# Four value loads ahead of the first relayout, and the first two relayouts issued from two queues

## The chip, the cores and the metric

The kernel runs on one core of a Trainium2 chip. The metric is the device time of one execution in microseconds, and a kernel is described by the median of several executions. Before the change that median is 673.52 us over three runs (673.15 to 676.69).

## The reference, cut to what matters

Talking-heads attention feeds two feed-forward blocks; all inputs and outputs are float32.

```
scores = 0.125 * q @ k.T                  # 2 batches, 12 heads, 448 x 448, head size 64
scores = einsum('bhij,hg->bgij', scores, w_pre)       # mixes the 12 heads
attn   = softmax(scores, axis=-1)
attn   = einsum('bhij,hg->bgij', attn, w_post)        # mixes the 12 heads again
x      = (attn @ v)  as 896 tokens x 768
x      = (silu(x @ w_gate) * (x @ w_val)) @ w_out     # 768 -> 1536 -> 768
h      = x @ w_in                                     # 768 -> 2048
y      = (h * clip(h + 3, 0, 6) / 6) @ w_out2         # 2048 -> 768
```

## The kernel before, in words

The attention is worked off in eight tiles `t` of 100 to 120 query rows, four for each batch. For a tile, `scores` multiplies q and k for six pairs of heads (`c` = 0 to 5), and `scores_out` copies the two banks of a pair to a tile `S` in SBUF, one by VectorE (DVE) and one by ScalarE (ACT). In `S` a partition is a query row, and the heads lie beside each other. To mix the heads on TensorE they have to lie on partitions. That is the **relayout**: a DMA inside SBUF takes every twelfth row of `S` and writes each head of such a row to a partition of its own in a tile `sx`. A chunk is ten query rows. `relayout(m)` moves eight of its rows (104 partitions of `sx`, L204, issued by SyncE, called SP here), `relayout_rest(m)` the other two (24 partitions, L220, issued by GpSimd, called POOL). I call them relayout m and rest m. There are 90 chunks, and two chunks make one `sx` tile and one **step** i; 45 steps follow each other. `S` exists twice, so tile 0 is in one and tile 1 in the other.

Step i works on several stages at once: `premix(i+2)` (L239, TensorE multiplies `sx` by the first mixing matrix), `row_max(i+2)` (L252, DVE), `exps(i+1)` (L261, ACT), `weights(i+1)` (L269 to L273, DVE), `postmix(i)` (L287, TensorE), `attn_out(i)` (L306, DVE and ACT), and, spread over the steps, the scores of a later tile, attention times values (`av`, L318 and L337) and loads. The order of the instructions on each engine is the order in which this code is written; nothing reorders it. Each engine works its own list from the front, and an instruction that waits holds all that stands behind it on its engine. A DMA stands in the list of the engine that issues it.

DMAs that SP and ACT issue take eight semaphores in turn, named DMAHW0 to DMAHW7, in the order of the code. A DMA that takes a semaphore waits until the DMA that used it last, eight such DMAs earlier, has landed. POOL's DMAs have eight others (DMASW). `next_engines` is a DMA of a few bytes that POOL issues between groups of four rests.

At the start, q and k of tile 0 are loaded in pieces from SP and ACT, then q of tiles 1 and 2, both mixing matrices (`W1`, `W2`) and the first two of four pieces of the first batch's values (`load_v(0, j)`, L118) from SP. TensorE computes all scores of tiles 0 and 1 (L526 to L536); between the two tiles the code issues relayouts 0 to 7. Then the steps begin at i = -2. The other two value pieces are issued by ACT at the ends of steps 1 and 2, and q of tile 3 (`load_q`, L109) by ACT at the end of step 3. Relayouts 8 and later are placed by the rules in L650 to L657: at most three in a step, no more than a few steps ahead, and only if the tile was scored in an earlier step (`scored`).

Of the kernel before, what the change touches and what calls it, by code (L numbers as in the profile page):

```python
# [16 lines left out]
B, H, S, D = 2, 12, 448, 64  # L17
NT = B * S
DM = H * D
HP = H // 2  # L20
# [7 lines left out]
JC = 4  # L28
# [20 lines left out]
def kernel(  # L49
# [14 lines left out]
    nc = tc.nc  # L64
# [5 lines left out]
    def bank(name, tag):  # L70
        return ps.tile([128, 512], F32, name=name, tag=tag, bufs=BUFS[tag])
# [18 lines left out]
    small = kp.tile([128, 8], F32, name="small")  # L90
# [23 lines left out]
    def new_v(b):  # L114
        vs[b] = pv.tile([128, JC, H, D], F32, name=f"v{b}", tag="v")

    def load_v(b, j, eng=nc.scalar):
        eng.dma_start(  # L118
            out=vs[b][:, j].rearrange("p h d -> p (h d)"), in_=vv[b, :, j * DM : (j + 1) * DM]
        )  # L120
# [15 lines left out]
    nc.sync.dma_start(out=W2.rearrange("p g k -> p (g k)"), in_=w_post)  # L136
    load_q(2, eng=nc.sync)
    new_v(0)
    for j in range(2):
        load_v(0, j, nc.sync)  # L140

    Ss = [psc.tile([128, H + 1, S], F32, name=f"S{i}") for i in range(2)]
# [14 lines left out]
    stiles, pqk = {}, {}  # L157

    def scores(t, c, tags=("pqk", "pqk")):

        b, i = divmod(t, 4)
        n = ROWS[b][i]
        if c == 0:
            stiles[t] = Ss[t % 2]
        base = c * n
        p = [bank(f"pqk{t}_{c}_{e}", tags[e]) for e in range(2)]
        for s in range(2):
            lo, hi = 64 * s, min(64 * s + 64, n)
            for e in range(2):
                r = slice(64 * e, 64 * e + 64)  # L170
                nc.tensor.matmul(  # L171
                    p[e][lo:hi, :S],
                    lhsT=qs[t][r, base + lo : base + hi],
                    rhs=ks[b][r, c, :],
                    start=True,
                    stop=True,
                    tile_position=(64 * e, 64 * s),
                )
        for e in range(2):
            pqk[t, 2 * c + e] = p[e]  # L180

    def scores_out(t, c):
        n = ROWS[t // 4][t % 4]
        for e in range(2):
            h = 2 * c + e
            copy = nc.scalar.copy if e else nc.vector.tensor_copy
            copy(stiles[t][:n, h, :], pqk.pop((t, h))[:n, :S])  # L187

    sx = {}

    in_turn = mybir.DependencyInfo(mybir.DependencyClass.Sync, mybir.DependencyReason.DATA)

    def relayout(m, then=None):

        t, c = chunks[m]
        i, r = divmod(m, 2)  # L200
        if r == 0:
            sx[i] = psx.tile([128, 2, S], F32, name=f"sx{i}", tag="sx")
        rows = stiles[t][c : c + 7 * STRIDE + 1 : STRIDE, :, :]
        dma = nc.sync.dma_start(out=sx[i][0:104, r, :], in_=rows)  # L204
        if then:
            tc.add_manual_dep(dma.ins, then, in_turn, reason="a step's share of the DMA engines")

    def next_engines(n):

        to = 4 + n % 4  # L210
        nc.gpsimd.dma_start(
            out=small[0:24, to : to + 1], in_=small[0:8, 0:3].rearrange("p (h w) -> p h w", w=1)
        )

    next_engines(0)

    def relayout_rest(m):
        t, c = chunks[m]
        rows = stiles[t][c + 8 * STRIDE : c + 9 * STRIDE + 1 : STRIDE, :H, :]
        nc.gpsimd.dma_start(out=sx[m // 2][104:128, m % 2, :], in_=rows)  # L220
        if m % 4 == 3 and m + 1 < NCH:
            next_engines(m // 4 + 1)

# [105 lines left out]
    turns = cst.tile([1, 1], F32, name="turns")  # L329
# [189 lines left out]
    def keep_clock(n):  # L519

        p = ps.tile([128, 512], F32, name=f"clock{n}", tag="ppost", bufs=BUFS["ppost"])
        for _ in range(n):
            nc.tensor.matmul(p[:, :480], lhsT=ones[0], rhs=ones[1], start=True, stop=True)

    keep_clock(WARM)
    placed = 0  # L526
    for t in range(2):
        for c in range(HP):
            scores(t, c, (("pqk", "pqk"), ("ppre", "ppre"), ("ppost", "ppost"), ("ppre", "pav"))[(6 * t + c) % 4])
            scores_out(t, c)  # L530
        if t == 0:
            for _ in range(8):
                relayout(placed)
                relayout_rest(placed)
                placed += 1
    rests = placed  # L536

# [3 lines left out]
    def at_step(i, f, *args, place="end"):  # L541
        extra[i][place].append((f, args))
# [9 lines left out]
        else:  # L552
            at_step(now + 1, scores_out, t, c, place="S")

    scored = {0: -3, 1: -3}
    for t in range(2, 8):
        scored[t] = 6 * t - 7
        for c in range(HP):
            i = scored[t] - 5 + c
# [8 lines left out]
    for t, (begin, end) in enumerate(((5, 10), (11, 16), (17, 22), (23, 28), (29, 34), (35, 40), (41, 46))):  # L568
        busy = None
        for c in range(HP):  # L570
            i = begin + c * (end - begin + 1) // HP
            out = x_out if t < 6 else x_last
# [11 lines left out]
        if t < 6:  # L584
            step = 1 if t < 4 else 2
            i = split_at.setdefault(t, max(end + 1, split_at.get(t - 1, 0) + 4 // step))
# [4 lines left out]
    at_step(20, new_v, 1)  # L591
    for b in range(2):
        at_step(scored[4 * b + 3] + 1, new_x, b)
    loads = [(1, load_v, 0, 2), (2, load_v, 0, 3), (3, load_q, 3), (6, load_q, 4)]
    loads += [(7 + n, load_k, 1, n, n + 1) for n in range(HP)]
    loads += [(15, load_q, 5), (21, load_q, 6), (27, load_q, 7)]
    loads += [(20 + 2 * j, load_v, 1, j) for j in range(JC)]
# [17 lines left out]
    for i in range(-LOOK, NP):  # L615
# [36 lines left out]
        for m in ready[:1]:  # L652
            relayout(m, begun_at)
        run(i, "end")
        for m in ready[1:]:
            relayout(m, maxed)
        placed += len(ready)  # L657

        while rests < placed and rests // 2 <= i + LOOK + 4 and i > scored[chunks[rests][0]]:
            relayout_rest(rests)  # L660
            rests += 1
# [181 lines left out]
```

## Time and profile before

| | |
|---|---|
| median of three runs | 673.52 us |
| the profiled execution, its own time | 671.94 us |
| span in its profile | 670.2 us |
| TensorE busy | 659.1 us (98% of the span) |
| VectorE, ScalarE, GpSimd busy | 499.8, 296.5, 160.4 us |
[...]

The span is the time from the first to the last instruction on the chip. The profiled execution took 1.74 us more than its span, and 1.58 us less than the median. "PE" is TensorE's multiplications and "PEld" its weight loads; "SPq" and "ACTq" are the instructions with which SP and ACT issue DMAs. In a row of the timeline, the bracket says how long the engine stood idle before, and who ended that.

### The profile page before, as it was taken

What the parts mean: (1) busy time and instruction counts of PE and PEld (TensorE: products, weight loads), DVE (VectorE), ACT (ScalarE), POOL (GpSimd) and SP (SyncE); (2) the same over time, 40 slices, a digit from 0 to 9 for tenths busy, and PEclk for the clock granted to TensorE, in tenths of its full rate; (3) what the DMA queues carried; (4) which work ended last, traced back from release to release, by engine and by line L of the source; (5) the groups of instructions that cost most, each with busy time, mean ns of one, the idle gap of its engine ahead of it and who ended that gap; (6) DMA issues with size and microseconds to landing.
All of it is one profiled execution on the core that took longest, in us unless ns stands there. A gap on an engine that the chain in (4) does not pass through costs nothing.

```text
span 670.2 us, 16126 instructions
## 1 busy us (share of the span) xinstructions
PE 659.1 (98%) x6680; PEld 561.8 (84%) x6680; DVE 499.8 (75%) x836; ACT 296.5 (44%) x603; POOL 160.4 (24%) x204
## 2 busy tenths in 40 slices
PE   8999999999999999999999999999999999999997
PEld 2456665666899999999999999999999998999996
DVE  4878888889278888887886666578888888775540
ACT  4567776777244343433432323244445543333220
POOL 3544466545111122111120000013333332000000
PEclk9999999999999999999999999999999999999999
DMA  7767576545024242332432434222223333554420
GB/s 253 218 200 210 178 219 192 181 142 198 3 94 141 95 141 95 112 124 95 135 100 95 132 104 134 102 94 97 94 95 101 119 96 100 178 155 122 145 67 27
DMA packets 35225, 86.87 MB, mean 130 GB/s; under 512 B 10096, under 2 KB 23040, under 8 KB 35152
## 3 DMA queue, kind: packets, MB, share of 16 engines
q1 hardware_dynamic: 21600, 71.43, 32.3%
q10 hardware_dynamic: 5616, 10.48, 5.1%
q0 software_dynamic: 7936, 3.94, 2.4%
q8 instruction: 52, 0.85, 0.6%
q14 instruction: 21, 0.17, 0.1%
HBM read 62.37 MB, written 2.75 MB: 97 GB/s over the span
## 4 chain that ended last, share of the span: by engine, by line
PE 94%; DMA 3%; DVE 2%; ACT 1%; issue 0%; ACTq 0%; SPq 0%; DVEq 0%
PE pi L441 17%; PE pp L441 17%; PE po L441 13%; PE pv L441 12%; PE pg L441 12%; PE pav L318 5%; PE ppost L287 5%; PE ppre L239 4%; PE pqk L171 4%; PE p L441 2%; PE pav L337 2%; DMA sx<-S 2%; DMA k<-in_k_dram 1%; ACT e L261 1%; DVE nm L252 0%
## 5 line engine op out<-in xcount | busy, mean ns | idle before, releaser
L441 PE MATMUL pp<-g,hp 128*128 128x448 f32 x384 | 107.9, 362 | 0.0
L703 POOL TENSOR_TENSOR g<-rl,g 128x448 fp32r<-128x448 f32 x32 | 41.4, 1313 | 167.9 <-ACT g L702 167.9
L441 PE MATMUL po<-u,ho 128*128 128x448 f32 x288 | 81.3, 363 | 0.0
L441 PEld LDWEIGHTS pp<-g,hp 128*128 128x128 f32 x384 | 71.9, 187 | 4.5 <-ACT hp L427 0.2
L261 ACT ACTIVATE e<-ppre,nm 128x448 f32<-128x448 f32 x90 | 56.3, 631 | 35.4 <-DVE nm L252 33.8
L441 PE MATMUL pp<-g,lp 128*128 128x448 f32 x192 | 69.7, 363 | 0.2 <-DVE lp L432 0.2
L441 PE MATMUL pi<-x2l,hi 128*128 128x448 f32 x192 | 69.7, 363 | 0.0
L441 PE MATMUL pi<-x2h,hi 128*128 128x448 f32 x192 | 69.6, 362 | 0.0
L441 PE MATMUL pi<-x2h,li 128*128 128x448 f32 x192 | 69.1, 360 | 0.0
L703 POOL TENSOR_TENSOR u<-sg,u 128x448 fp32r<-128x448 f32 x24 | 32.2, 1362 | 148.3 <-ACT u L702 148.3
L220 POOL DMA_DIRECT2D sx<-S x90 | 52.5, 584 | 49.5 <-issue 11.8
L441 PEld LDWEIGHTS po<-u,ho 128*128 128x128 f32 x288 | 54.1, 188 | 3.5
L252 DVE TENSOR_REDUCE nm<-ppre 128x1 f32<-128x448 f32 x90 | 51.9, 618 | 4.8 <-PE ppre L239 2.3
L287 PE MATMUL ppost<-wn,e 60*64 60x60 f32 x2520 | 51.0, 220 | 3.0 <-DVE wn L273 1.7
L441 PE MATMUL po<-u,lo 128*128 128x448 f32 x144 | 51.8, 360 | 0.0
L318 PEld LDWEIGHTS pav<-at,v 128*64 128x64 f32 x576 | 27.9, 136 | 28.4 <-ACT xs L360 14.2
L239 PE MATMUL ppre<-sx,W 64*64 64x448 f32 x360 | 49.7, 544 | 1.3 <-ACT S L187 0.6
L287 PEld LDWEIGHTS ppost<-wn,e 60*64 60x64 f32 x2520 | 45.1, 134 | 6.1 <-ACT at L306 2.0
L171 PE MATMUL pqk<-k,q 64*64 64x448 f32 (+3 forms) x384 | 47.8, 539 | 1.2 <-DMA k<-in_k_dram 0.6
L441 PE MATMUL pg<-xl,hg 128*128 128x448 f32 x132 | 47.9, 363 | 0.0
L441 PE MATMUL pv<-xl,hv 128*128 128x448 f32 x132 | 47.9, 363 | 0.0
L441 PE MATMUL pg<-xh,hg 128*128 128x448 f32 x132 | 47.8, 362 | 0.0
(98 smaller groups left out, 1399.1 us busy)
## 6 DMA issues: line engine op xcount, KB each, us to landing
sx<-S SPq DMA_DIRECT2D x90, 182.0 KB
ri<-in_moe_w_in_dram SPq DMA_DIRECT2D x16, 768.0 KB
ro<-in_moe_w_out_dram SPq DMA_DIRECT2D x12, 768.0 KB
rg<-in_moe_w_gate_dram SPq DMA_DIRECT2D x11, 768.0 KB
rv<-in_moe_w_val_dram SPq DMA_DIRECT2D x11, 768.0 KB
rp<-in_moe_w_out_dram SPq DMA_DIRECT2D x12, 640.0 KB
rp<-in_moe_w_out_dram SPq DMA_DIRECT2D x6, 768.0 KB
sx<-S POOLq DMA_DIRECT2D x90, 42.0 KB, 4.5
```

The source lines that it names most:

```text
L171: nc.tensor.matmul(p[e][lo:hi, :S], lhsT=qs[t][r, base + lo : base + hi], rhs=ks[b][r, c, :], start=True, stop=True, tile_position=(64 * e ...
L220: nc.gpsimd.dma_start(out=sx[m // 2][104:128, m % 2, :], in_=rows)
L239: nc.tensor.matmul(p[a][64 * r : 64 * r + 64, :S], lhsT=W1[rows, :], rhs=x[rows, r, :], start=True, stop=True, tile_position=(64 * a, 64 * r),
L252: top = nc.vector.tensor_reduce(nm[:, a : a + 1], pre[i][a][:, :S], AX.X, ALU.max, negate=True)
L261: nc.scalar.activation(e2[a], p[a][:, :S], AF.Exp, bias=nm[:, a : a + 1], scale=1.0, accum_out=sm[:, a : a + 1])
L287: mm = nc.tensor.matmul(p[s][64 * c : 64 * c + 64, at, :, :], lhsT=e2[a][rows, 64 * k : 64 * k + 64], rhs=wn[rows, a, :].rearrange("p (g k ...
L318: nc.tensor.matmul(p[64 * e : 64 * e + 64, : 2 * n], lhsT=vs[b][:, jc, h, :], rhs=ats[t][:, 2 * jc : 2 * jc + 2, h, :n], start=jc == 0, st ...
L337: mm = nc.tensor.matmul(pavs[t, c][64 * e : 64 * e + 64, a * n : a * n + n], lhsT=vs[b][rows, JC - 1, h, :], rhs=ats[t][rows, KB - 1, h, : ...
L441: nc.tensor.matmul(p[:, :S], lhsT=wt[:, kk, :], rhs=xx, start=start, stop=stop)
L703: eng.tensor_tensor(to[1], src, to[0].bitcast(F32), ALU.subtract)
```

## The change

All four pieces of the first batch's values are now loaded by SP ahead of the first relayout; the two loads that ACT issued in steps 1 and 2 are gone. Relayout 1 is issued by ACT and rest 0 by SP. The last pair of scores of tile 1 is computed behind the first premix, and its copies stand behind the first exponentials; the relayouts of tile 1 may therefore start only in step 0 and not in step -1. The banks of the scores of tiles 0 and 1 are listed one by one so that the first premix finds free banks. The first `next_engines` moves 16 elements where it moved 24.

```
-    for j in range(2):
+    for j in range(JC):
         load_v(0, j, nc.sync)
...
-    def relayout(m, then=None):
+    def relayout(m, then=None, eng=nc.sync):
...
-        dma = nc.sync.dma_start(out=sx[i][0:104, r, :], in_=rows)
+        dma = eng.dma_start(out=sx[i][0:104, r, :], in_=rows)
...
-    def next_engines(n):
+    def next_engines(n, turns=3):
...
-            out=small[0:24, to : to + 1], in_=small[0:8, 0:3].rearrange("p (h w) -> p h w", w=1)
+            out=small[0 : 8 * turns, to : to + 1], in_=small[0:8, 0:turns].rearrange("p (h w) -> p h w", w=1)
...
-    next_engines(0)
+    next_engines(0, 2)
...
-        nc.gpsimd.dma_start(out=sx[m // 2][104:128, m % 2, :], in_=rows)
+        eng.dma_start(out=sx[m // 2][104:128, m % 2, :], in_=rows)
...
+    banks = [("pqk", "pqk"), ("ppre", "ppre"), ("ppost", "ppost"), ("ppre", "pav"), ("pqk", "pqk"), ("ppre", "ppre")]
+    banks += [("ppost", "ppost"), ("ppre", "pav"), ("pqk", "pqk"), ("ppost", "ppost"), ("pqk", "pqk"), ("ppost", "ppost")]
     for t in range(2):
         for c in range(HP):
-            scores(t, c, (("pqk", "pqk"), ("ppre", "ppre"), ("ppost", "ppost"), ("ppre", "pav"))[(6 * t + c) % 4])
+            if (t, c) == (1, HP - 1):
+                break
+            scores(t, c, banks[6 * t + c])
             scores_out(t, c)
         if t == 0:
             for _ in range(8):
-                relayout(placed)
-                relayout_rest(placed)
+                relayout(placed, eng=nc.scalar if placed == 1 else nc.sync)
+                relayout_rest(placed, eng=nc.sync if placed == 0 else nc.gpsimd)
                 placed += 1
...
-    scored = {0: -3, 1: -3}
+    scored = {0: -3, 1: -1}
+    at_step(-2, scores, 1, HP - 1, banks[-1], place="av2")
+    at_step(-1, scores_out, 1, HP - 1, place="S")
...
-    loads = [(1, load_v, 0, 2), (2, load_v, 0, 3), (3, load_q, 3), (6, load_q, 4)]
+    loads = [(3, load_q, 3), (6, load_q, 4)]
```

SP's list at the start, before the change, with the semaphores that each DMA waits for: two value loads, then relayouts 0 to 3 (two to a tile `sx`).

```order
L109 DMA q2_114<-in_q_dram 128x720 [waits DMAHW4_49]
L118 DMA v0_116<-in_v_dram 128x768 [waits DMAHW5_49]
L118 DMA v0_116<-in_v_dram 128x768 [waits DMAHW6_49]
L204 DMA sx0_187<-S0_119 104x1x448 [waits DVE_49,DMAHW7_49,Activation_49,Pool_49]
L204 DMA sx0_187<-S0_119 104x1x448 [waits DMAHW0_49]
L204 DMA sx1_192<-S0_119 104x1x448 [waits DMAHW1_49]
L204 DMA sx1_192<-S0_119 104x1x448 [waits DMAHW2_49]
```

The same place of SP's list with the change; L220 is rest 0.

```order
L109 DMA q2_114<-in_q_dram 128x720 [waits DMAHW4_49]
L118 DMA v0_116<-in_v_dram 128x768 [waits DMAHW5_49]
L118 DMA v0_116<-in_v_dram 128x768 [waits DMAHW6_49]
L118 DMA v0_116<-in_v_dram 128x768 [waits DMAHW7_49]
L118 DMA v0_116<-in_v_dram 128x768 [waits DMAHW0_49]
L204 DMA sx0_189<-S0_121 104x1x448 [waits DVE_49,DMAHW2_49,Activation_49,Pool_49]
L220 DMA sx0_189<-S0_121 24x1x448 [waits DMAHW3_49]
L204 DMA sx1_194<-S0_121 104x1x448 [waits DMAHW4_49]
L204 DMA sx1_194<-S0_121 104x1x448 [waits DMAHW5_49]
```

Four value loads stand ahead of relayout 0 instead of two, rest 0 stands behind it, and relayout 1 has left for ACT's list.

ACT's list in steps 1 to 3 before the change: `S0` copies of tile 2's scores (L187), the two value loads, q of tile 3 with its semaphore, and the exponentials of steps 3 to 5 (L261).

```order
L118 DMA v0_116<-in_v_dram 128x768
L261 ACTIVATE e2_126,sm3_413<-ppre3_0_389,nm3_395 128x448 [waits DVE_49,Activation_49]
L261 ACTIVATE e3_127,sm3_413<-ppre3_1_390,nm3_395 128x448 [waits DVE_49,Activation_49]
L306 COPY at0_327<-ppost2_1_417 128x84x5 [waits PE_49]
L187 COPY S0_119<-pqk2_1_1_463 120x448 [waits PE_49]
L118 DMA v0_116<-in_v_dram 128x768 [waits DMAHW2_49]
L261 ACTIVATE e0_124,sm4_476<-ppre4_0_453,nm4_459 128x448 [waits DVE_49,Activation_49]
L261 ACTIVATE e1_125,sm4_476<-ppre4_1_454,nm4_459 128x448 [waits DVE_49,Activation_49]
L306 COPY at0_327<-ppost3_1_480 128x84x5 [waits PE_49]
L187 COPY S0_119<-pqk2_2_1_526 120x448 [waits PE_49]
L109 DMA q3_535<-in_q_dram 128x714 [waits DMAHW5_49]
L261 ACTIVATE e2_126,sm5_541<-ppre5_0_516,nm5_522 128x448 [waits DVE_49,Activation_49]
```

The end of the same stretch with the change.

```order
L306 COPY at0_323<-ppost2_1_418 128x84x5 [waits PE_49]
L187 COPY S0_121<-pqk2_1_1_464 120x448 [waits PE_49]
L261 ACTIVATE e0_126,sm4_476<-ppre4_0_454,nm4_460 128x448 [waits DVE_49,Activation_49]
L261 ACTIVATE e1_127,sm4_476<-ppre4_1_455,nm4_460 128x448 [waits DVE_49,Activation_49]
L306 COPY at0_323<-ppost3_1_480 128x84x5 [waits PE_49]
L187 COPY S0_121<-pqk2_2_1_526 120x448 [waits PE_49]
L109 DMA q3_535<-in_q_dram 128x714 [waits DMAHW6_49]
L261 ACTIVATE e2_126,sm5_541<-ppre5_0_516,nm5_522 128x448 [waits DVE_49,Activation_49]
```

The value loads are gone, and q of tile 3 waits for another semaphore. Who held these two semaphores stands in SP's list; before the change, DMAHW5 is relayout 14's, the first of `sx7`:

```order
L204 DMA sx6_344<-S1_120 104x1x448 [waits DMASW2_49,DMAHW3_49,DMASW1_49,PE_49]
L204 DMA sx6_344<-S1_120 104x1x448 [waits DMAHW4_49,DVE_49]
L204 DMA sx7_406<-S1_120 104x1x448 [waits DMASW4_49,DMAHW5_49,DMASW3_49,PE_49]
L204 DMA sx7_406<-S1_120 104x1x448 [waits DMAHW6_49,DVE_49]
L204 DMA sx8_470<-S1_120 104x1x448 [waits DMASW7_49,DMAHW0_49,DMASW6_49,PE_49]
```

With the change, DMAHW6 is relayout 12's, the first of `sx6`, and relayouts 10 to 12 stand together:

```order
L204 DMA sx4_266<-S0_121 104x1x448 [waits DMAHW3_49,DVE_49]
L204 DMA sx5_340<-S1_122 104x1x448 [waits DVE_49,PE_49,DMAHW4_49,Activation_49,Pool_49]
L204 DMA sx5_340<-S1_122 104x1x448 [waits DMAHW5_49,DVE_49]
L204 DMA sx6_343<-S1_122 104x1x448 [waits DMAHW6_49,DMASW1_49]
L204 DMA sx6_343<-S1_122 104x1x448 [waits DMAHW7_49,PE_49]
L204 DMA sx7_407<-S1_122 104x1x448 [waits DMASW3_49,DMAHW0_49,DMASW2_49,DVE_49]
```

So the DMA that q of tile 3 has to wait for is two relayouts earlier than before, and relayouts 10 and 11 now wait for the postmix and the row maximum of a later step (PE and DVE in their waits).

## Rows read from the trace of the kernel before

**Rows 1.** Page, the chain that ended last: shares of the span by engine.

```profile
PE 94%; DMA 3%; DVE 2%; ACT 1%; issue 0%; ACTq 0%; SPq 0%; DVEq 0%
```

**Rows 2.** Busy time by stretch: stretch, its length, busy time (instructions), clock, DMA share, GB/s.

```profile
34.00:170.00 136.00, 132.94 (x3616) 85.87 (x3616) 115.58 (x338) 97.83 (x281) 70.73 (x117) 1.00 0.61 187
170.00:670.00 500.00, 496.03 (x2602) 463.37 (x2600) 362.70 (x451) 181.01 (x283) 74.94 (x58) 1.00 0.33 107
```

**Rows 3.** The chain that ended last, 10 to 38 us: start, us, what.

```profile
11.84 4.36 DMA sx<-S
16.25 0.98 PE ppre L239 x4
17.91 1.35 ACT e L261 x4
...
25.35 7.85 DMA sx<-S
33.23 0.33 ACTq L109
```

**Rows 4.** Timeline of TensorE at the first premix.

```profile
15.26 4.01 PE L239 MATMUL ppre<-sx,W 64*64 64x448 f32 x16 [0.64 <-ACT S L187]
16.25 0.30 PEld L239 LDWEIGHTS ppre<-sx,W 64*64 64x64 f32 x6 [0.83 <-DMA sx<-S]
```

**Rows 5.** DMA engines, 7 to 12.4 us: mean busy tenths in 40 slices; issues and KB.

```profile
DMA  7889999999999999995778979999999664327100
v<-in_v_dram SPq DMA_DIRECT2D x2, 384.0 KB
sx<-S SPq DMA_DIRECT2D x2, 182.0 KB
sx<-S POOLq DMA_DIRECT2D x2, 42.0 KB, 3.6
```

**Rows 6.** DMA engines, 8.4 to 11.4 us: totals; queue: packets, MB, share of 16 engines.

```profile
DMA packets 418, 1.01 MB, mean 336 GB/s; under 512 B 85, under 2 KB 85, under 8 KB 418
q1 hardware_dynamic: 402, 1.01, 96.3%
```

**Rows 7.** DMA engines, 12.4 to 24 us: SP's and ACT's hardware queue.

```profile
q1 hardware_dynamic: 1163, 1.94, 47.1%
```

**Rows 8.** Timeline of SP's issues: relayouts 0 to 17 merged, and relayout 5 alone.

```profile
10.95 19.27 SPq L204 DMA_DIRECT2D sx<-S  x18
15.30 1.12 SPq L204 DMA_DIRECT2D sx<-S  x1
```

**Rows 9.** Timeline of VectorE, steps -2 to 0.

```profile
17.25 1.16 DVE L252 TENSOR_REDUCE nm<-ppre 128x1 f32<-128x448 f32 x2 [1.95 <-PE ppre L239]
19.28 0.17 DVE L269 TENSOR_SCALAR rc<-sm 128x2 f32<-128x2 f32 x1 [0.88 <-ACT e L261]
22.52 1.15 DVE L252 TENSOR_REDUCE nm<-ppre 128x1 f32<-128x448 f32 x2
```

**Rows 10.** Timeline of ScalarE: a copy of tile 1, then steps 2 and 3.

```profile
10.96 0.54 ACT L187 COPY S<-pqk 120x448 f32<-120x448 f32 x1 [0.21 <-PE pqk L171]
...
28.86 0.53 ACT L187 COPY S<-pqk 120x448 f32<-120x448 f32 x1 [0.84 <-PE pqk L171]
28.86 0.34 ACTq L118 DMA_DIRECT2D v<-in_v_dram  x1
29.30 0.63 ACT L261 ACTIVATE e<-ppre,nm 128x448 f32<-128x448 f32 x1
...
31.89 0.53 ACT L187 COPY S<-pqk 120x448 f32<-120x448 f32 x1 [0.77 <-PE pqk L171]
33.97 0.63 ACT L261 ACTIVATE e<-ppre,nm 128x448 f32<-128x448 f32 x1 [1.55 <-DVE at L306]
```

**Rows 11.** Timeline of TensorE at premix 2 and at premix 5.

```profile
20.95 0.97 PE L239 MATMUL ppre<-sx,W 64*64 64x448 f32 x8
29.45 1.22 PE L239 MATMUL ppre<-sx,W 64*64 64x448 f32 x6
```

More of the change, by code (lines that the diff above doesn't have):

```diff
@@ L203, in relayout, with relayout_rest @@
         rows = stiles[t][c : c + 7 * STRIDE + 1 : STRIDE, :, :]
-        dma = nc.sync.dma_start(out=sx[i][0:104, r, :], in_=rows)
+        dma = eng.dma_start(out=sx[i][0:104, r, :], in_=rows)
         if then:
             tc.add_manual_dep(dma.ins, then, in_turn, reason="a step's share of the DMA engines")
-    def next_engines(n):
+    def next_engines(n, turns=3):
         to = 4 + n % 4
         nc.gpsimd.dma_start(
-            out=small[0:24, to : to + 1], in_=small[0:8, 0:3].rearrange("p (h w) -> p h w", w=1)
+            out=small[0 : 8 * turns, to : to + 1], in_=small[0:8, 0:turns].rearrange("p (h w) -> p h w", w=1)
         )
-    next_engines(0)
-    def relayout_rest(m):
+    next_engines(0, 2)
+    def relayout_rest(m, eng=nc.gpsimd):
         t, c = chunks[m]
         rows = stiles[t][c + 8 * STRIDE : c + 9 * STRIDE + 1 : STRIDE, :H, :]
-        nc.gpsimd.dma_start(out=sx[m // 2][104:128, m % 2, :], in_=rows)
+        eng.dma_start(out=sx[m // 2][104:128, m % 2, :], in_=rows)
         if m % 4 == 3 and m + 1 < NCH:
```

## The prediction

> **What bounds the kernel now.** I read the page's chain first: TensorE has 94% of it, DMA 3%, the rest little [rows 1]. The table by stretch then says where TensorE is not the bound: from 34 us on it is busy 132.94 of 136 us and 496.03 of 500 us [rows 2]. So nearly all of what the change can touch lies before 34 us, and a shift of the front there passes on to the end one for one, because behind it an almost unbroken row of TensorE work follows. The chain between 10 and 38 us [rows 3] shows the front's two DMA waits. First, relayout 1 is issued at 11.84 us and holds the chain for 4.36 us; premix 0 runs on from 16.25 us. TensorE could have gone on earlier: it began premix 0 at 15.26 us and its weight loads then stood 0.83 us until the relayout came [rows 4]. Second, a relayout issued at 25.35 us lands 7.85 us later, and what waits is no premix but ACT's load of q for tile 3, at 33.23 us. By the order, that load takes the semaphore of relayout 14 and holds ACT's list until it has landed. Behind it stand the exponentials of step 5, which start at 33.97 us after 1.55 us of idle ACT [rows 5]; the copy before them ended at 31.89 + 0.53 = 32.42 us. The bracket names DVE there, but by the chain the DMA issue came last.
>
> **The value loads ahead of relayout 0 (cost).** Two loads of 384 KB (393,216 bytes each) [rows 6] are added to SP's list ahead of the first relayout. In SP's list they cost nothing: the next thing there waits until 10.95 us for the copies of tile 0 [rows 7], and the semaphores they take were last used by early pieces of q and k. On the DMA engines they cost time. While the first two value loads ran, the queue kept 96.3% of the 16 engines busy at 336 GB/s [rows 8], so two more take 786,432 / 336,000 = 2.34 us. Part of that is free, since the engines run dry before relayout 0 now begins: the last nine slices of 0.135 us up to 12.4 us are busy 6, 6, 4, 3, 2, 7, 1, 0 and 0 tenths, which leaves 6.1 slices, 0.82 us, idle [rows 6]. Net +1.52 us for the data of relayout 0. Bounds: 0, if the relayouts pass the loads without loss, and +2.34 us, if none of the idle time is filled.
>
> **Relayouts 0 and 1 side by side (no gain).** Before, relayout 1 was issued 11.84 - 10.95 = 0.89 us after relayout 0 [rows 3, 7]; now both go at 10.95 us. But from 12.4 to 24 us the queue keeps 47.1% of 16, that is 7.5, engines busy with relayouts alone and moves 1.94 MB [rows 9], or 10.4 relayouts of 182 KB (186,368 bytes): 1.11 us for each. Were the idle half usable by a relayout, the share would not stay at half while SP has the next ones issued. [...] By the rows, the gain lies between 0 and the 0.89 us between the issues; I take 0, since the engines that carry relayouts were full.
>
> **Rest 0 on SP's list.** It stands behind relayout 0 and ahead of relayout 2. By its bytes it adds 42/182 of 1.11 = 0.26 us [rows 6, 9]; at most a whole relayout's 1.11 us. It feeds the second half of premix 0 alone, whose row maximum is second of two that take 1.16 us [rows 10], so 0.58 us of it is hidden. I take 0 for the chain and keep +0.5 as an upper end. Relayouts 2 to 7 stand behind both, later by 1.5 to 1.8 us. The next that matters is relayout 5, for premix 2. At the pace above it lands about four relayouts after relayout 1: 16.20 + 4.4 = 20.6 us, an estimate from [rows 3, 9], and premix 2 starts at 20.95 us [rows 11]. With 1.8 us on the one and 1.5 us on the other they stay level: no further cost, up to +0.3.
>
> **The issue on ACT.** SP's issues take about 1.07 us each (18 in 19.27 us) [rows 7]; ACT's copies of tile 1 move from 10.96 us to about 12, and stood 0.21 us idle each before [rows 5]. Five of them need 2.7 us and are done near 15 us, before premix 0 can start. The cover is the relayout's landing; without it this would cost 1 us.
>
> **The moved scores.** The last pair of tile 1 costs TensorE nothing where it stood (its premix waited for a DMA) and nothing where it goes (behind premix 0 it waits for the exponentials). Its DVE copy fits the 0.88 us of idle time before the reciprocals [rows 10], its ACT copy of 0.54 us the time between exponentials 17.91 + 1.35 = 19.26 us and the next row maximum. Relayouts 10 and 11 slip a step: relayouts 11 and 12 follow the row maximum that ended at 22.52 + 1.15 = 23.67 us [rows 10], now about 25.2 and 26.2 us. With 4.36 us to land, relayout 11 is there at 29.6 us, while premix 5 starts at 29.45 + 1.5 = 31.0 us [rows 11]. With 7.85 us, it would be late by 2.0 us.
>
> **The loads taken off ACT (gain).** Their issue cost ACT nothing: it ran beside a copy, and the exponentials followed 0.44 us after that copy's start [rows 5]. But they are counted among the eight semaphores and they filled DMA engines while relayout 14 was due. Now q of tile 3 waits for relayout 12, issued near 26.2 us and there by 30.5 us (34.0 at the slow pace); ACT comes to it near 33.9 us. So the stall goes: -1.55 us, bounds -1.64 (were the exponentials to follow 0.44 us after the copy's start, as in step 2) and 0. What is late next there is the row maximum of step 5, which the order has ready in time.
>
> **The pool's engines.** [...] I take 0.
>
> **Sum.** +1.52 + 0 + 0 + 0 - 1.55 = -0.03 us on the profiled execution's 671.94 us: 671.9 us. The median of the runs shown is 1.58 us higher, so I forecast 673.5 us.
>
> **Rivals.** (1) Side by side pays: the loads are hidden (0), the issue gap is saved (-0.89) and the stall goes (-1.55): -2.4 us, 671.1 us. For it: relayouts fill only half of the engines, and ACT's queue need not stand behind the value loads. Against: rest 0 and relayout 0 still stand behind them, and premix 0 needs both. (2) The loads push and the stall stays: +2.34 + 0.3 and no gain, +2.6 us, 676.1 us. It decides if relayout 12 takes as long as relayout 14 did, so that ACT still stands at q of tile 3; for it is relayout 12's later issue, against it that no value load competes any more. (3) The slip of relayouts 10 and 11 becomes the wait: premix 5 stands for them 2.0 us, with the 1.5 us of the start and the stall replaced, not removed: +3.6 us, 677.1 us. It decides where relayout 11 needs more than 31.0 - 25.2 = 5.8 us to land. (4) The change does nothing at the end, because later idle time takes up any shift: TensorE's 3.1 and 4.0 us of idle time after 34 us [rows 2] would have to lie in waits for something that does not move with the front; the chain shows none of size, and the time would again be 673.5 us.
>
> **How the numbers follow.** Forecast (with rival 4, which gives the same time) 0.55; rival 1 0.20; rival 2 0.19; rival 3 0.06. The measurement tells about 0.5%, 3.4 us, from no change, that is 670.1 to 676.9 us. Rivals 1 and 2 lie inside; rival 3 lies just outside, and I give it 0.05 for slower; 0.03 for faster stands for gains that I have not priced. The forecast's own range is 672.3 to 674.7 us. The whole range goes to 671.0 and 676.1 us, the two rivals.
>
> **What would show it.** Premix 0's main part starts near 17.8 us instead of 16.25; the exponentials of step 0 near 19.4 instead of 17.91. ACT's idle time before the exponentials of step 5 falls from 1.55 us to a few tenths, and q of tile 3 is issued beside a copy. The steps after 34 us are as long as before, and the front there stands within 1 us of where it stood. The forecast is wrong if premix 0 starts at or before 16.25 us, if ACT still stands at q of tile 3, if premix 2 or 5 waits for a relayout by more than 0.5 us, or if the steps behind 40 us change their length.

## The result, and the profile after

The changed kernel takes 678.34 us (median, 675.52 to 681.13) against 673.26 us of the kernel before on the same chip (670.20 to 676.69), 16 runs each: a ratio of 1.0077, 95% interval 1.0062 to 1.0092. I forecast no change (673.5 us, range 671.0 to 676.1); it is slower, and outside the range. The profiled execution took 679.65 us, with a span of 677.8 us.

An erratum first. From 5 on, the group numbers in the prediction are mixed up: what it cites as rows 5 is group 10 of the list (ScalarE), its 6 is group 5, its 7 is 8, its 8 is 6, its 9 is 7 and its 10 is 9. Groups 1 to 4 and 11 are cited rightly. Below, the numbers are those of the list.

The chain of the page gives TensorE less than before [rows 1]:

```profile
PE 92%; DMA 3%; DVE 2%; issue 1%; POOL 0%; ACT 0%; SPq 0%; DVEq 0%; POOLq 0%
```

The two stretches of [rows 2], with one ahead of them: stretch, its length, busy time (instructions) of PE, PEld, DVE, ACT, POOL, then clock, DMA share, GB/s.

```profile
16.25:34.00 17.75, 15.61 (x304) 7.49 (x304) 12.33 (x33) 10.00 (x27) 9.70 (x17) 0.90 0.58 189
34.00:170.00 136.00, 131.22 (x3495) 83.33 (x3495) 113.25 (x325) 93.11 (x268) 65.19 (x111) 0.99 0.58 176
170.00:670.00 500.00, 499.22 (x2784) 465.37 (x2775) 367.70 (x468) 185.50 (x295) 79.82 (x63) 1.00 0.33 109
```

From 34 to 170 us TensorE executes 3,495 instructions where it executed 3,616: it falls behind inside this stretch, and DMA moves 176 GB/s where it moved 187. And the granted clock, 1.00 before in all three stretches, is no longer 1.00 throughout (0.90 and 0.99 in the first two; over the whole span 0.994, before 1.000). How far the front has fallen behind, read from the start of each step's first exponential (L261):

| step | before, us | after, us | behind by |
|---|---|---|---|
| 0 | 17.91 | 19.20 | 1.29 |
| 1 | 20.54 | 23.27 | 2.73 |
| 4 | 29.30 | 32.00 | 2.70 |
| 5 | 33.97 | 35.05 | 1.08 |
| 11 | 53.73 | 54.80 | 1.07 |
| 13 | 60.38 | 65.05 | 4.67 |
| 23 | 94.57 | 99.99 | 5.42 |
| 24 | 98.10 | 105.60 | 7.50 |
| 44 | 165.25 | 173.25 | 8.00 |

So at 54 us the account stood near what I had worked out, 1.07 us behind, and nearly 7 us were lost after that, in a few steps and not in all. These are two single executions: the one before is 1.3 us under its kernel's median, the one with the change 1.3 us over it, and the profile of a variant with a ratio of 1.000 (below, two `next_engines` more) stands 2.83 us behind at step 44. What a gap of 2 or 3 us in one profile is worth has to be read from the variants.

The start. The chain of the changed kernel (start, us, what; compare [rows 3]):

```profile
10.70 6.14 DMA sx<-S
16.84 0.14 issue
16.98 2.22 PE ppre L239 x6
...
21.50 0.61 DVE S L187
...
23.27 1.35 ACT e L261 x4
```

Relayout 0 needs 6.14 us behind four value loads, and premix 0 (2.22 us for six of its products) starts 1.72 us later than its first instructions did in [rows 4]. The timeline of TensorE shows the idle time ahead of it, and the table by stretch the clock behind it (columns as above):

```profile
13.77 0.98 PE L171 MATMUL pqk<-k,q 64*64 64x448 f32 x8
16.98 2.22 PE L239 MATMUL ppre<-sx,W 64*64 64x448 f32 x6 [2.23 <-DMA sx<-S]
```

```profile
18.00:21.50 3.50, 3.50 (x19) 1.42 (x20) 1.26 (x3) 1.45 (x4) 2.27 (x4) 0.51 0.66 209
...
58.00:62.40 4.40, 2.19 (x80) 1.66 (x76) 2.42 (x8) 2.43 (x7) 0.75 (x2) 1.00 0.76 232
62.40:65.80 3.40, 3.30 (x16) 1.10 (x16) 1.16 (x2) 0.75 (x3) 0.00 (x0) 0.50 0.27 91
```

Twice, at the end of over 2 us for which TensorE had stood or about 1 us later, the granted clock falls to 0.50 of full speed for some 3.4 us. The first time this falls on the end of premix 0, premix 1 and the moved scores; their copy (21.50 us in the chain) then stands between step 0's exponentials and step 1's, and the 1.29 us become 2.73. The nearest comparison is the changed kernel with the first `next_engines` at its old size (below): by the landings in the traces its relayout 1 was there at 17.26 us, here at 17.33; its clock stayed at 1.00, and it was 1.06 us behind at step 0 and at step 1.

Four steps later 1.6 us of it come back. ScalarE's timeline around q of tile 3 (compare [rows 10], where it stood 1.55 us):

```profile
34.59 0.53 ACT L187 COPY S<-pqk 120x448 f32<-120x448 f32 x1 [0.76 <-PE pqk L171]
34.60 0.34 ACTq L109 DMA_DIRECT2D q<-in_q_dram  x1
35.05 0.63 ACT L261 ACTIVATE e<-ppre,nm 128x448 f32<-128x448 f32 x1
```

The load is issued beside a copy, and the exponentials of step 5 follow 0.46 us after that copy's start. The stall is gone, as I had forecast.

The largest single loss, at step 13, in the timeline of TensorE:

```profile
59.94 0.26 PE L337 MATMUL pav<-at,v 64*64 64x60 f32 x2
62.50 1.88 PE L239 MATMUL ppre<-sx,W 64*64 64x448 f32 x8 [2.31 <-DMA sx<-S]
```

The bracket names a relayout, but by the landings in the trace both relayouts and rests of this premix were there by 56.8 us. What did land in between is a packet of the queue that the profile calls `q8 instruction`, from 59.93 to 60.96 us. I call such a packet a block, and take it for a block of TensorE's own instructions; what speaks for that stands in the last section. The DMA view of 59.9 to 61.0 us (queue: packets, MB, share of 16 engines) shows it:

```profile
q1 hardware_dynamic: 70, 0.12, 29.1%
q10 hardware_dynamic: 47, 0.08, 19.0%
q8 instruction: 1, 0.02, 5.9%
```

From its landing to TensorE's next instruction it is 1.54 us. The same pair is in the chain of the kernel before, once, as 1.31 us of "issue" at 102.51 us, with a block that landed at 102.31 us, 1.51 us ahead of the next instruction.

This loss is no mark of the slow variants. The changed kernel with three more small DMAs on POOL's list (below), whose median of 674.95 us is not measurably slower than before, has the same gap in its profile, also with half clock behind it, and stands 4.92 us behind at step 14; that execution took 677.46 us.

```profile
61.97 1.09 PE L242 MATMUL ppre<-sx,W 64*64 64x448 f32 x8 [2.21 <-DMA sx<-S]
```

### The profile page after: what moved, and what is told of

The parts are those of the page before. It is cut to its first block, busy times and chain, and to the rows that moved or that the text cites. A ratio compares the mean times of both kernels' runs of the same rounds, so it can differ in the third digit from the quotient of the medians.

```text
span 677.8 us, 16124 instructions
## 1 busy us (share of the span) xinstructions
PE 662.5 (98%) x6680; PEld 563.8 (83%) x6680; DVE 500.6 (74%) x836; ACT 296.4 (44%) x603; POOL 159.7 (24%) x203
## 4 chain that ended last, share of the span: by engine, by line
PE 92%; DMA 3%; DVE 2%; issue 1%; POOL 0%; ACT 0%; SPq 0%; DVEq 0%; POOLq 0%
PE pi L441 17%; PE pp L441 17%; PE po L441 13%; PE pv L441 12%; PE pg L441 12%; PE ppre L239 5%; PE ppost L287 4%; PE pqk L171 4%; PE pav L318 4%; DMA sx<-S 2%; PE p L441 2%; PE pav L337 2%; DMA k<-in_k_dram 1%; DVE nm L252 1%; DVE S L187 0%
## 5 line engine op out<-in xcount | busy, mean ns | idle before, releaser
L261 ACT ACTIVATE e<-ppre,nm 128x448 f32<-128x448 f32 x90 | 56.3, 630 | 41.6 <-DVE nm L252 41.5
L220 POOL DMA_DIRECT2D sx<-S x89 | 51.8, 582 | 62.8 <-DVE rc L269 13.8
L239 PE MATMUL ppre<-sx,W 64*64 64x448 f32 x360 | 52.2, 562 | 5.3 <-DMA sx<-S 4.5
L171 PE MATMUL pqk<-k,q 64*64 64x448 f32 (+3 forms) x384 | 51.8, 558 | 1.5 <-ACT S L187 0.8
L441 PE MATMUL pv<-xh,hv 128*128 128x448 f32 x132 | 47.8, 362 | 0.0
```

The source lines that it names most:

```text
L171: nc.tensor.matmul(p[e][lo:hi, :S], lhsT=qs[t][r, base + lo : base + hi], rhs=ks[b][r, c, :], start=True, stop=True, tile_position=(64 * e ...
L220: eng.dma_start(out=sx[m // 2][104:128, m % 2, :], in_=rows)
L239: nc.tensor.matmul(p[a][64 * r : 64 * r + 64, :S], lhsT=W1[rows, :], rhs=x[rows, r, :], start=True, stop=True, tile_position=(64 * a, 64 * r),
L261: nc.scalar.activation(e2[a], p[a][:, :S], AF.Exp, bias=nm[:, a : a + 1], scale=1.0, accum_out=sm[:, a : a + 1])
L441: nc.tensor.matmul(p[:, :S], lhsT=wt[:, kk, :], rhs=xx, start=start, stop=stop)
```

## Experiments

Each variant was timed in five rounds beside the kernel before. For all of them I also took, from the landings in the trace, the mean time from issue to landing of the relayouts issued between 40 and 110 us (35 to 42 of them): 5.44 us before the change, 6.50 us with it.

**One part at a time.** Loads alone:

```
-    for j in range(2):
+    for j in range(JC):
...
-    loads = [(1, load_v, 0, 2), (2, load_v, 0, 3), (3, load_q, 3), (6, load_q, 4)]
+    loads = [(3, load_q, 3), (6, load_q, 4)]
```

> The kernel before, with one part of the change alone: all four value loads on SP ahead of relayout 0. Theory A (the time behind 40 us is lost to late instruction blocks of TensorE, because the rests now use other DMA engines): this part moves no rest, so premix 0 starts 1 to 2 us later, the exponentials of step 5 lose their 1.5 us stall, and the time is 673 us, ratio 1.000 within 0.002; no new TensorE gap of 2 us behind 40 us. Theory B (the loads cost it all: TensorE stands over 2 us ahead of premix 0, comes back at half clock, and the shifted front meets the later transfers badly): ratio 1.005 or more, half clock right behind premix 0's start.

Measured: 674.78 us, ratio 1.0031 (1.0003 to 1.0059), relayouts 5.74 us. Step 4 is 1.70 us behind and step 5 is 0.06: what was lost up to there the stall gives back. That is the size of my sum's cancellation, but in part by luck. Only 0.69 us are lost at step 0; 1.02 us follow at step 3, where the variant with two `next_engines` more, which has none of these loads, loses 1.33 us too. The median is 2.1 us up, more than the 0.002 that theory A allowed, with an interval that nearly reaches nothing; where that arises its profile, 0.66 us behind at step 44, does not show.

The queue part alone (relayout 1 on ACT, rest 0 on SP, the shorter first next_engines):

```
-    next_engines(0)
+    next_engines(0, 2)
...
-                relayout(placed)
-                relayout_rest(placed)
+                relayout(placed, eng=nc.scalar if placed == 1 else nc.sync)
+                relayout_rest(placed, eng=nc.sync if placed == 0 else nc.gpsimd)
```

> The kernel before, with the queue part alone: relayout 1 from ACT, rest 0 from SP, 16 elements in the first turn of POOL's engines. Theory A: the rests' DMA engines shift here too, so TensorE meets gaps of 1 to 2 us behind 40 us that end as an instruction block lands; ratio 1.004 to 1.007 (676 to 678 us). Theory B: nothing but the first premix changes, by 0.5 us or less: ratio 1.000.

Measured: 679.43 us, ratio 1.0085 (1.0055 to 1.0115), relayouts 6.37 us. This part alone is as slow as the whole change. Theory A expected the gaps to end as a block of instructions lands; two do end behind such a landing (at 126.94 and 166.25 us). What TensorE waits for in the three others shows in the rows of VectorE around 46, 68 and 110 us:

```profile
46.38 0.62 DVE L187 COPY S<-pqk 119x448 f32<-119x448 f32 x1 [1.47 <-DMA small<-small]
...
68.46 0.62 DVE L187 COPY S<-pqk 120x448 f32<-120x448 f32 x1 [2.40 <-DMA sx<-S]
...
110.72 0.62 DVE L187 COPY S<-pqk 119x448 f32<-119x448 f32 x1 [1.63 <-DMA sx<-S]
```

Each is the first copy of a new tile's scores into an `S` that an older tile's last relayouts and rests still read; it must wait until they have landed (the first bracket names the small DMA of `next_engines`, the others a relayout or rest). `S` exists twice, and the landings had little to spare: before the change the copy at 64.30 us began 0.7 us after the last relayout that reads its `S` had landed. TensorE then waits for VectorE:

```profile
69.17 0.27 PE L337 MATMUL pav<-at,v 64*64 64x60 f32 x2 [1.69 <-DVE turns L348]
```

The moved scores alone:

```
-    scored = {0: -3, 1: -3}
+    scored = {0: -3, 1: -1}
+    at_step(-2, scores, 1, HP - 1, banks[-1], place="av2")
+    at_step(-1, scores_out, 1, HP - 1, place="S")
```

> The kernel before, with the moved scores alone: the last pair of tile 1 behind premix 0, its copies a step later, relayouts of tile 1 from step 0. Both theories: premix 0 as before (it waits for relayout 1), ratio 1.000 within 0.002. A third theory C, that the slip of relayouts 10 and 11 costs, expects 1.003 (2 us) with premix 5 waiting for a relayout.

Measured: 673.26 us, ratio 1.000 (0.9976 to 1.0024), relayouts 5.57 us. By themselves they cost nothing that these runs can tell, as I had said.

**Putting the rests back.** What of the queue part does it? One rest fewer is on POOL's list, so every later rest comes one place earlier among POOL's DMAs. That this gives them other DMA engines is what theory A assumes; no trace shows the engine of a DMA. The changed kernel plus one small DMA in the place of the missing rest:

```
     next_engines(0, 2)
+    nc.gpsimd.dma_start(out=small[0:4, 3:4], in_=small[0:2, 1:3].rearrange("p (h w) -> p h w", w=1))
```

> The changed kernel, with one DMA of a few bytes over two partitions added on POOL in the place where rest 0 stood, so that rests 1 and later use the DMA engines again that they used before the change (if POOL deals its DMAs to engines in turn). Theory A: the gaps behind 40 us go and the time comes back to 674 us, ratio to the kernel before 1.001. Theory B: as the changed kernel, 678 us, ratio 1.007.

Measured: 674.96 us, ratio 1.0027 (1.0000 to 1.0053), relayouts 5.62 us. A DMA of a few bytes takes back some two thirds of the loss; theory A had expected all but 0.1%. TensorE's row from 34 to 170 us is at the level of before again (in an execution of 671.37 us, the second fastest of its twelve):

```profile
34.00:170.00 136.00, 133.83 (x3632) 86.02 (x3628) 116.36 (x339) 97.59 (x280) 69.53 (x115) 1.00 0.61 183
```

**Moving the rests, with nothing else changed.** The kernel before with the same small DMA:

```
     next_engines(0)
+    nc.gpsimd.dma_start(out=small[0:4, 3:4], in_=small[0:2, 1:3].rearrange("p (h w) -> p h w", w=1))
```

> [...] Theory A (the loss of the changed kernel comes from the rests' place among the DMA engines): slower by 0.4 to 0.9%, relayouts between 40 and 110 us land about 0.5 to 1 us later than before, and the gaps of TensorE lie between 40 and 170 us. Rival B (the loss comes from the start: relayout 1 on ACT's list and rest 0 on SP's): within 0.2% of before, since the start is as it was.

Measured: 680.16 us, ratio 1.0116 (1.0079 to 1.0153), relayouts 6.74 us. More than expected, and the start theory (B) is refuted. The chain of this variant at 66 to 71 us:

```profile
66.80 2.69 DMA sx<-S
69.50 0.00 issue
69.50 0.62 DVE S L187
70.12 0.03 DVE rc L270
70.16 0.04 issue
70.20 0.27 PE pav L338 x2
```

It is the same wait as in the queue part alone: a landing, the copy into `S`, VectorE's next instructions, TensorE. TensorE stood 2.01 us for it.

A second `next_engines`:

```
     next_engines(0)
+    next_engines(3)
```

> [...] Rival B (the loss comes from the start alone): within 0.2% of before. [...]

Measured: 684.45 us, ratio 1.0173 (1.0142 to 1.0203), slower still, and B is refuted here too. But the relayouts land after 6.71 us, as with the small DMA (6.74 us): the mean is no finer measure than "disturbed or not". In this variant one relayout also brings back the wait of ScalarE for q of tile 3, larger than before; its chain at 33 to 40 us:

```profile
27.80 9.60 DMA sx<-S
37.40 0.02 issue
37.42 0.33 ACTq L109
```

**Is it the place, or the extra DMA?** The kernel before with two extra DMAs, which are once two `next_engines` and once two of the small DMAs:

```
     next_engines(0)
+    next_engines(2)
+    next_engines(3)
```

> [...]

```
     next_engines(0)
+    for at in (3, 7):
+        nc.gpsimd.dma_start(out=small[0:4, at : at + 1], in_=small[0:2, 1:3].rearrange("p (h w) -> p h w", w=1))
```

> [...]

Measured: with two `next_engines`, 674.37 us, ratio 1.000 (0.9978 to 1.0022), relayouts 5.32 us; with two small DMAs, 682.96 us, ratio 1.0133 (1.0100 to 1.0166), relayouts 6.93 us. The number of extra DMAs and the turn of the semaphores are the same, so neither makes the difference. What the two kinds of DMA change for the rests behind them, no trace shows. With two small DMAs the copy into `S` waits longest of all, 3.70 us, and soon after it, from 72.34 us, the granted clock is 0.50 for 3.4 us: 3.23 us are lost at step 15 and 1.60 us more at step 16. The chain at 67 to 72 us:

```profile
67.72 3.04 DMA sx<-S
70.76 0.03 issue
70.79 0.62 DVE S L187
71.42 0.10 DVE rc L271
71.51 0.25 PE pav L339 x2
```

The changed kernel with the small DMA in the place of the missing rest and two `next_engines` more:

```
     next_engines(0, 2)
+    next_engines(2)
+    next_engines(3)
+    nc.gpsimd.dma_start(out=small[0:4, 3:4], in_=small[0:2, 1:3].rearrange("p (h w) -> p h w", w=1))
```

> [...] Rival F (the number of POOL's DMAs or the turn of its semaphores): 1.007 or more.

Measured: 674.95 us, ratio 1.0012 (0.9987 to 1.0037), relayouts 5.86 us, below the 1.007 of F. And the changed kernel with the first `next_engines` at its old size:

```
-    next_engines(0, 2)
+    next_engines(0)
```

> The changed kernel with the first next_engines at 24 elements again, as before the change. [...] Theory A: as slow as the changed kernel, ratio 1.005 to 1.010 to before. [...]

Measured: 678.27 us, ratio 1.0076 (1.0047 to 1.0104), relayouts 6.69 us: the size does nothing that can be told, so that of the two edits to POOL's list it is the missing rest that costs. This variant, whose rests stand as in the changed kernel, shows the copy's wait too:

```profile
66.69 0.62 DVE L187 COPY S<-pqk 120x448 f32<-120x448 f32 x1 [2.49 <-DMA small<-small]
```

ScalarE's copy beside it, at 66.42 us, stood 1.31 us, and there the bracket names a relayout or rest.

In the changed kernel's own profile this wait does not show. The first copy over the `S` of tile 2, before and with the change, neither with a wait:

```profile
64.30 0.62 DVE L187 COPY S<-pqk 120x448 f32<-120x448 f32 x1
69.62 0.61 DVE L187 COPY S<-pqk 120x448 f32<-120x448 f32 x1
```

By the landings the last relayout that reads this `S` took 6.19 us before (57.40 to 63.59 us) and 8.41 us with the change (58.70 to 67.11 us). With the front as at step 11 the copy would have come at 64.30 + 1.07 = 65.37 us and waited some 1.7 us, an estimate; the gap at step 13 had held it up for longer. A copy into `S` that by its bracket stood over 1 us for a DMA, between 40 and 175 us, is in five of the fourteen profiles, all five of the second group below, and in none of the eight of the first.

So the fourteen kernels fall into two groups by what POOL's list has. The first has it as in the kernel before or with the small DMA in the place of the missing rest, in both cases also with two `next_engines` more: ratios are 0.9996 to 1.0031 and the relayouts' means 5.25 to 5.86 us. The second lacks a rest with nothing in its place, or has one or two small DMAs or one `next_engines` more: 1.0076 to 1.0173 and 6.37 to 6.93 us. I call the rests of the first group in place and those of the second moved. The two groups do not touch, though the intervals at their edges (up to 1.0059, and from 1.0047) do. Nor does the half clock explain the difference: among the executions with a mean granted clock of 0.999 or more the median is 677.88 us for the queue part alone (3 of 7) against 672.00 us for the kernel before beside it (21 of 30), and 676.22 us for the changed kernel (5 of 16). Theory A's explanation, the rests' place among the DMA engines, is not shown: the trace has no engine numbers. What the runs show is which DMAs ahead of the rests cost: one small one 1.0116, two of them 1.0133, one `next_engines` 1.0173, and two `next_engines` nothing, 1.000.

**The change without its queue part:** loads and moved scores alone.

```
     next_engines(0)
...
                 relayout(placed)
                 relayout_rest(placed)
```

> The changed kernel with relayouts 0 and 1 and rests 0 and 1 on the lists of the kernel before, and the first next_engines with 24 elements again: the four value loads and the moved scores are all that is left of the change. Theory A: the loss of the queue part is gone, ratio to before 1.001 to 1.004, near that of the loads alone. Rival E (the parts need each other, the moved scores slip relayouts 10 and 11 and cost with the later start): 1.006 or more.

Measured: 672.90 us, ratio 1.0019 (0.9992 to 1.0045), relayouts 5.25 us. Against 1.0027 with the queue part and the rests put back, relayouts 0 and 1 side by side gain nothing that can be told. In its profile step 5 stands 1.60 us ahead of before, step 30 3.34 us ahead, and step 31 0.36 us: one gap took 2.71 us, in the chain at 118 us:

```profile
118.34 2.71 issue
121.05 0.27 PE ppost L287 x2
```

A block (queue q8) landed at 119.55 us, 1.50 us ahead of the next instruction.

**A faster version?** The one gain that was clear, the wait of ScalarE, without the loads:

```
-    loads = [(1, load_v, 0, 2), (2, load_v, 0, 3), (3, load_q, 3), (6, load_q, 4)]
+    loads = [(1, load_v, 0, 2), (2, load_v, 0, 3), (3, load_q, 3, 0, HP, nc.sync), (6, load_q, 4)]
```

> The kernel before, with one edit: q of tile 3 is issued by SP instead of ACT at the same step. ACT's list then no longer stands behind relayout 14's semaphore. If the 1.5 us of idle ScalarE ahead of the exponentials of step 5 was on the path that sets the end, the time falls by 1 to 1.6 us, ratio 0.9976 to 0.9985, and the exponentials of step 5 start 1.0 to 1.6 us earlier. Rival: the wait only moves to SP's list, where it holds the relayouts behind it, and the gain is lost within the next steps: ratio 1.000.

Measured: 672.53 us, ratio 0.9996 (0.9972 to 1.0021). The wait is gone: step 5 starts at 31.03 us, 2.94 us ahead of before, where steps 0 to 4 were some 1.3 us ahead. But at step 13 1.33 us are left and at step 44 0.68 us. The time is as the rival had it: gained there, given back within the next steps. Its reason, that SP's wait holds up the relayouts, is not shown. The chain shows where the first 0.71 us went, at step 9, and it is the copy into `S` again, which waits for a rest issued at 37.07 us (there at 42.28 us by the landings):

```profile
37.07 4.58 DMA sx<-S
...
42.65 0.62 DVE S L187
43.27 0.04 DVE rc L269
43.30 0.04 issue
43.35 0.26 PE pav L337 x2
```

TensorE stood 0.78 us there. So with the rests in place, too, this copy can be the next wait when the front comes earlier. No version beat both kernels measurably.

## Why the prediction was wrong

**The step that failed: "The pool's engines", taken as 0.** No run shows this term, since no trace gives the engine of a DMA. What the runs show in its place is that the missing rest costs (the size of `next_engines` does nothing), and where: the relayouts land later, after 6.50 us on average where it was 5.44, and what has no slack for that is the copy that overwrites `S`, and TensorE behind it. That path is seen in five variants; in the one profile of the changed kernel the copy came too late to meet it, so for this kernel it is argued from the landings and from the medians. The queue part alone has a ratio of 1.0085, and one small DMA with nothing else 1.0116. At 1.0077 minus 1.0027, a small DMA in the place of the missing rest is worth some 0.5% of the time, or 3.4 of the 5.1 us. The rest of the loss, at the edge of the noise, the runs give to no part of the change. I should have bounded it as I did the other unseen costs.

**The rule that a shift of the front passes on one for one.** It failed in both directions. Behind 40 us I saw TensorE busy 132.94 of 136 us [rows 2] and took the rest to be out of reach. But how late DMAs land decides there how long a step takes (from step 14 to 15 it is 3.40 us before the change, and 5.63 us with one small DMA more), and the lead of the front was given back in two profiles (with q of tile 3 on SP, in part to the copy into `S`; with loads and moved scores, in the one gap of 2.71 us). A busy share of 98% told how much idle time there was, not how near other waits stood. What else took the gain of q of tile 3 on SP, behind step 9, is open.

**The start (term +1.52 us).** Near in size. By the landings relayout 0 came 1.72 us later than before (16.84 against 15.12 us), relayout 1 1.13 us later (17.33 against 16.20), and the last rest of premix 0, now rest 0, 1.56 us later (18.14 against 16.58); the exponentials of step 0 came 1.29 us later, at 19.20 us, where I had said 19.4. What I missed is the clock: at a granted clock of 0.51 premix 1 and the moved scores, which stand on the chain there, made 2.73 us of it at step 1. The moved scores, taken as 0, are 0 by themselves (ratio 1.000).

**The ScalarE wait (-1.55 us).** Right in mechanism and size: 2.70 us behind at step 4, 1.08 at step 5, so -1.62.

**The issue on ACT (0).** Mis-sized, though it did not decide. The row of this issue and the next copy in the changed kernel:

```profile
10.71 1.56 ACTq L204 DMA_DIRECT2D sx<-S  x1
12.31 1.40 ACT L187 COPY S<-pqk 120x448 f32<-120x448 f32 x3 [1.82 <-PE pqk L171]
```

It held ACT 1.56 us, where I counted about 1; the copies were done near 15.4 us, still ahead of premix 0.

**Side by side (0).** Nothing speaks against it: with the rests in place the pair gains nothing that can be told (1.0027 with it, 1.0019 without). But each interval is some 1.8 us either way, so that the 0.89 us of my bound are not ruled out.

**The rivals.** None named the cause. Rivals 2 and 3 came near in time (676.1 and 677.1 us) for reasons that did not occur: ScalarE did not stand at q of tile 3, and relayouts 10 and 11 held up nothing. The sign I gave for a wrong forecast, that the steps behind 40 us change their length, is what happened.

## What to carry to other kernels

When a DMA is taken off a queue, ask what that does to all later ones on it, and time the kernel once with a small DMA in the place of the one removed: here that took the ratio from 1.0077 to 1.0027. Read slack at a reused buffer from the landing of its last reader to the first write after it, not from the reader's own consumer. And do not take a busy share of 98% as proof that a gain upstream reaches the end: one experiment that removes a single wait shows how much of it arrives.

## What had not been expected of the hardware

The page of the kernel before lists a queue `q8 instruction` with 52 packets, 0.85 MB and 0.6% of the 16 engines' span, beside the queues that move the data. In eleven gaps of over 1 us ahead of 170 us, in nine of the fourteen profiles, TensorE went on 1.45 to 1.62 us after such a block had landed, whatever wait the bracket named. That these blocks are TensorE's instructions is an inference, from this and from the place of the gaps: counted with those of its sequencer, TensorE's instructions ahead of such a gap are 2,241 in the changed kernel and 4,545 in the kernel before, and in all eleven gaps the number is 193 over a multiple of 256. The trace of the kernel before has 13,452 of them, or 259 for each of the 52 packets, an estimate of what a block holds. Five of the nine profiles have the rests in place.

The granted clock fell to 0.50 for 3.4 us at or soon after the end of idle times of TensorE of 2.23 and 2.31 us in the changed kernel, while the loads alone, with 2.08 us ahead of premix 0, kept 1.00. It does not follow from the idle time alone: the 2.71 us of the loads with moved scores were followed by a clock of 1.00, and in the variant with two `next_engines` more 2.41 us of it, to 105.92 us, were too.

```profile
105.90:109.40 3.50, 3.48 (x97) 2.48 (x99) 2.25 (x5) 1.65 (x5) 1.88 (x4) 1.00 0.46 80
```
